# A gated linear scan with a feed-forward layer: a list scheduler that counts TensorE's changes of mode and searches 1,000 orders

## The chip, the cores and the metric

The kernel runs on one core of one Trainium2 chip. The core has five engines that run side by side, each strictly in the order of its own instruction list: TensorE (PE, matrix products; its weight loads are listed apart as PEld), VectorE (DVE, elementwise work and scans), ScalarE (ACT, activation functions and copies), GpSimd (POOL) and SyncE (SP, which here issues every transfer). An instruction waits until the data it reads is there, and everything behind it on the same engine waits too. The metric is the time of one execution on the device in microseconds. The kernel before took 576.96, 577.83 and 579.1 us in three runs, median 577.83.

## The reference, cut to what matters

```python
# 4 batches, 8 heads, 768 positions, head size 48
scale = np.minimum(mag, 0.999) / (mag + 1e-06)       # mag = |a_re + i a_im|
a_re_n, a_im_n = (a_re * scale, a_im * scale)
for t in range(S):                                    # a gated state of 48x48 per head
    new_re = ar * S_re - ai * S_im
    new_im = ar * S_im + ai * S_re
    S_re, S_im = (new_re + k[t] v[t]^T, new_im)
    y[t] = q[t] @ S_re
x = y reshaped to 3072 tokens x 384
h = x @ w_in                                          # 384 -> 2048
g = np.where(h >= 1, h, np.where(h <= -1, 0.0, (h + 1) ** 2 / 4))
out = g @ w_out                                       # 2048 -> 384
```

All inputs and the output are float32.

## The kernel before, in words

**Tiling.** The 3072 tokens are cut into 12 units of 256 tokens (`u`). A unit passes three steps. `gates(u)` turns the gates into running log-magnitudes and angles and multiplies them into keys and queries; this is DVE and ACT work, and its last two products per unit (`turn`, line 834 before) write the tiles `x` and `kq`, whose rows are then moved to the per-head tiles `hd` by ten transfers (`spread`). `attend(u)` does the scan in chunks of 128 tokens on PE: `scores` (line 989, tile `sc`), `transposes` (933, `tp`), `products` (962, `dp`) and `values` (1030 and 1038, `yp`). DVE multiplies the scores by a mask (997, `am`); ACT copies `yp` to `xr` (1050), and six small transfers per unit move rows inside `xr`. `moe(blk)` is the feed-forward layer for a block of two units. `split` rounds `xr` into a high part `xH` (ACT, 1130) and a rest `xL` (DVE, 1137); `gemm1` (1160) multiplies with `w_in` into `h`, `gemm2` (1235) with `w_out` into `o`, each product as three matmuls of 128x512 (high-high, low-high, high-low). Between the two, ACT makes `s` (1185, and for the first two blocks also 1195 and 1199) and DVE makes `g` (1204, later also 1212); `gh` (ACT, 1218) and `gl` (DVE, 1222) are its two parts. The weights arrive packed and are unpacked on the way (`weights`: DVE lines 431, 440, 449, 460, ACT line 455). Attention of the later units is woven into the feed-forward work of the block before, in visits of a few matmuls.

**Width.** `values` and `products` run PE on 64 of its columns (the forms 96x64 and 128x64 in the profile), everything else on 128. Going from one to the other is what the change calls a change of mode.

**What sets the order.** Nothing is written out by hand. Every piece of work is recorded with `Plan.op`: its engine, a cost in ns, what it reads and writes, and, for some, a due time. `Plan.order` first walks backwards through the dependences, so that each piece gets the latest due time that its successors allow (DVE and ACT costs are taken 1.6 times for that). Then it plays the list forward once on five engines: the engine that is free first takes, among what is ready, the piece with the earliest due time. All pieces are emitted in the order of their planned starts. Tiles are single buffers with fixed places, so a writer also waits for the readers of the tile that lay there before.

**Fillers.** Where the plan shows a gap on PE ahead of the feed-forward part, `warm` puts matmuls into it whose result nobody reads (line 1290, `idle`; 85% of the planned gap at 224 ns for each).

Of the kernel before, what the change touches and what calls it, by code (L numbers as in the profile page):

```python
# [3 lines left out]

# [16 lines left out]
NH = 8  # L21
# [7 lines left out]
CH = 128  # L29
# [53 lines left out]
LO_PE = 3  # L83
INFLATE = 1.6
SPLIT_DUE = 3000


def key_rows():
# [36 lines left out]
class Plan:  # L125
# [3 lines left out]
    def __init__(self):  # L129
        self.ops = []  # L130
        self.slots = {}
        self.glued = {}
        self.loose = set()

    def tile(self, slot, make):
        t = Tile_(make, self.slots.get(slot))
        self.slots[slot] = t
        return t

    def op(self, eng, cost, fn, r=(), w=(), due=None, dma=0, after=(), glue=None, late=0):  # L140
        i = len(self.ops)
        pre = set(after)
# [24 lines left out]
        return i  # L167

    def order(self):
        ops = self.ops  # L170
        n = len(ops)
        succ = [[] for _ in range(n)]
        for i, o in enumerate(ops):
            for p in o[3]:
                succ[p].append(i)
        due = [0.0] * n
        big = 1e12
        for i in range(n - 1, -1, -1):
            eng, cost, _, _, d, dma, late = ops[i]
            t = big if d is None else d  # L180
# [4 lines left out]
            for s in succ[i]:  # L185
                t = min(t, due[s] - own)
            due[i] = t
        left = [len(o[3]) for o in ops]
        ready = [0.0] * n
        end = [0.0] * n  # L190
        start = [0.0] * n
        free = {e: 0.0 for e in ("PE", "DVE", "ACT", "SP", "POOL")}
        wait = {e: [] for e in free}
        avail = {e: [] for e in free}
        queue = {}

        def enable(i):
            heapq.heappush(wait[ops[i][0]], (ready[i], i))

        for i in range(n):  # L200
            if not left[i]:
                enable(i)
        done = 0
        taken = set()
        forced = []
        while done < n:
            if forced:
                i = forced.pop()
                e = ops[i][0]
                t = max(free[e], ready[i])  # L210
            else:
                best = None
                for e in free:
                    while avail[e] and avail[e][0][1] in taken:
                        heapq.heappop(avail[e])
                    while wait[e] and wait[e][0][1] in taken:
                        heapq.heappop(wait[e])
                    if avail[e]:
# [42 lines left out]
            for s in succ[i]:  # L261
                left[s] -= 1
                lat = LAT[eng]
                if dma or s in self.loose:
                    lat = 0
                elif ops[s][0] == eng:
                    lat = SAME[eng]
                ready[s] = max(ready[s], end[i] + lat)
                if not left[s]:
                    enable(s)  # L270
# [3 lines left out]
        self.start, self.end, self.due = start, end, due  # L274
        return sorted(range(n), key=lambda i: (start[i], i))

    def emit(self, warm):
        order = self.order()
# [43 lines left out]
def gated_scan_moe(  # L322
# [575 lines left out]
    def attend(u):  # L898
# [25 lines left out]
        def transposes(c):  # L924
            cs = slice(c * CH, (c + 1) * CH)
            out = []
            for g in range(2):
                TP = bank([P, 4, HR], f"tp_{u}_{g}_{c}")
                KT = pl.tile(f"kT{g}", lambda g=g: keys[g])

                def run(g=g, TP=TP):
                    for i, h in enumerate(GROUPS[g]):
                        PE_.transpose(TP.get()[:, i, :], head(h)[:, 0, cs], ident[:HR, :HR])  # L933

                def tail(TP=TP, KT=KT):
# [10 lines left out]
                out.append((4 * 83, run, [hd[h // 3] for h in GROUPS[g]], TP, tail))  # L946
                carry.setdefault("kT", []).append(KT)
            return out

        def products(c):  # L950
# [23 lines left out]
                    fn = lambda: V_.tensor_tensor(ST.get(), old.get(), DP.get()[:HR], op=ALU.add)  # L974
                pl.op("DVE", dve(DM), fn, r=[DP] + ([old] if old else []), w=[ST])

            return [(NH * 124, run, [*kT, V_c[0]], DP, tail)]

        def scores(c):
            cs = slice(c * CH, (c + 1) * CH)  # L980
            out, ams = [], []
            for g in range(2):
# [21 lines left out]
                        w=[AM],  # L1004
                    )

                out.append((4 * pe32(CH), run, [hd[h // 3] for h in GROUPS[g]], SC, tail))
                ams.append(AM)
            return out, ams

        def values(c, ams, st):
# [5 lines left out]
            def part(prs):  # L1017
# [59 lines left out]
        def visit(parts):  # L1077
            reads = [x for p in parts for x in p[2]]
            last = None
            for n, (cost, run, r, psum, tail) in enumerate(parts):  # L1080
# [499 lines left out]
```

## Time and profile before

| | |
|---|---|
| three timed runs | 576.96, 577.83, 579.1 us |
| span of the profiled execution | 575.6 us, 9984 instructions |
| what lies around the span, against the median of the runs | 2.2 us |
| PE busy | 561.4 us (98%), 3922 matmuls |
| DVE busy | 434.5 us (75%) |
| ACT busy | 406.1 us (71%) |
| mean granted PE clock | 0.998 |

The page gives the busy share of each engine over the whole span, and the same in 40 slices. An average of 75% for DVE hides that it is nearly full early on and half idle at the end, so the span is best read stage by stage. A matmul's row counts from its start to its modelled end, and matmuls overlap: what a matmul costs is the distance from its start to the next one's start (for 128x512 some 0.23 us), not the 0.39 us of its row.

### The profile page before, as it was taken

What the parts mean: (1) busy time and instruction counts of PE and PEld (TensorE: products, weight loads), DVE (VectorE), ACT (ScalarE), POOL (GpSimd) and SP (SyncE); (2) the same over time, 40 slices, a digit from 0 to 9 for tenths busy, and PEclk for the clock granted to TensorE, in tenths of its full rate; (3) what the DMA queues carried; (4) which work ended last, traced back from release to release, by engine and by line L of the source; (5) the groups of instructions that cost most, each with busy time, mean ns of one, the idle gap of its engine ahead of it and who ended that gap; (6) DMA issues with size and microseconds to landing.
All of it is one profiled execution on the core that took longest, in us unless ns stands there. A gap on an engine that the chain in (4) does not pass through costs nothing.

```text
span 575.6 us, 9984 instructions
## 1 busy us (share of the span) xinstructions
PE 561.4 (98%) x3922; PEld 478.4 (83%) x3922; DVE 434.5 (75%) x625; ACT 406.1 (71%) x654; POOL 1.7 (0%) x20
## 2 busy tenths in 40 slices
PE   8999999999999999999999999999999999999995
PEld 7798978888888888888888888888888888888883
DVE  4999999999979498579589878887885544455452
ACT  7776799887998998975576666667643333369972
POOL 1000000000000000000000000000000000000000
PEclk9999999999999999999999999999999999999999
DMA  8676571773641614712601613402312200078811
GB/s 352 250 198 192 163 262 55 192 282 114 188 173 48 195 68 125 237 57 82 174 2 52 202 56 102 153 2 85 114 56 72 74 1 7 21 265 309 298 42 61
DMA packets 23527, 77.42 MB, mean 134 GB/s; under 512 B 4528, under 2 KB 10288, under 8 KB 23472
## 3 DMA queue, kind: packets, MB, share of 16 engines
q1 hardware_dynamic: 23472, 76.70, 40.8%
q8 instruction: 33, 0.54, 0.4%
q14 instruction: 22, 0.18, 0.1%
HBM read 51.90 MB, written 4.72 MB: 98 GB/s over the span
## 4 chain that ended last, share of the span: by engine, by line
PE 78%; DVE 12%; ACT 5%; DMA 2%; issue 1%; SPq 0%; ACTq 0%; DVEq 0%
PE o L1235 30%; PE h L1160 29%; PE sc L989 6%; PE yp L1038 3%; PE yp L1030 3%; PE dp L962 2%; PE tp L933 1%; PE idle L1290 1%; ACT ai L608 1%; DVE kq L725 1%; DMA xr<-xr 1%; DMA ai<-in_art_dram 1%; DVE g L1204 1%; ACT x L608 1%; DVE raw_i L440 1%
## 5 line engine op out<-in xcount | busy, mean ns | idle before, releaser
L1160 PE MATMUL h<-xH,wi 128*128 128x512 f32 x576 | 180.6, 395 | 1.2 <-DVE g L1204 0.9
L1235 PE MATMUL o<-gh,wo 128*128 128x512 f32 x576 | 180.4, 394 | 0.0
L1160 PEld LDWEIGHTS h<-xH,wi 128*128 128x128 f32 x576 | 106.2, 188 | 22.6 <-DVE g L1204 1.1
L1235 PEld LDWEIGHTS o<-gh,wo 128*128 128x128 f32 x576 | 106.3, 188 | 21.6 <-issue 0.7
L1204 DVE TENSOR_TENSOR g<-h,s 128x512 f32<-128x512 f32 x96 | 65.9, 687 | 63.1 <-ACT s L1185 45.6
L1160 PE MATMUL h<-xL,wi 128*128 128x512 f32 x288 | 112.6, 391 | 0.0
L1235 PE MATMUL o<-gl,wo 128*128 128x512 f32 x288 | 112.5, 391 | 0.0
L1185 ACT ACTIVATE s<-h,cst 128x512 f32<-128x512 f32 x96 | 65.7, 685 | 42.0 <-PE h L1160 38.9
L1218 ACT CAST gh<-g 128x512 fp32r<-128x512 f32 x96 | 59.1, 616 | 46.0 <-DVE g L1212 43.6
L1222 DVE TENSOR_TENSOR gl<-g,gh 128x512 fp32r<-128x512 f32 x96 | 66.0, 687 | 31.9 <-ACT gh L1218 31.8
L1160 PEld LDWEIGHTS h<-xL,wi 128*128 128x128 f32 x288 | 54.1, 188 | 12.1 <-DVE xL L1137 0.4
L1235 PEld LDWEIGHTS o<-gl,wo 128*128 128x128 f32 x288 | 54.1, 188 | 11.6
L608 ACT ACTIVATE ai<-ai 128x768 f32<-128x768 f32 x49 | 41.2, 843 | 19.1 <-DVE ai L777 8.6
L989 PE MATMUL sc<-hd 96*128 96x128 f32 x384 | 49.6, 278 | 0.0
L989 PEld LDWEIGHTS sc<-hd 96*128 96x128 f32 x384 | 47.0, 192 | 2.2
L1212 DVE SCALAR_TENSOR_TENSOR g<-s,g 128x512 f32<-128x512 f32 x64 | 44.2, 691 | 1.8
L1038 PE MATMUL yp<-am,V 128*64 128x128 f32 x384 | 35.5, 273 | 0.2 <-DVE am L997 0.2
L997 DVE TENSOR_TENSOR am<-sc,sums 128x512 f32<-128x512 f32 x48 | 32.5, 683 | 3.1 <-PE sc L989 2.8
L1290 PE MATMUL idle<-sums,ident 128*128 128x128 f32 x238 | 31.3, 291 | 1.7 <-POOL sums masks.py:66 1.7
L1030 PE MATMUL yp<-hd,st 96*64 96x128 f32 x320 | 32.1, 278 | 0.3 <-DVE am L997 0.3
L1290 PEld LDWEIGHTS idle<-sums,ident 128*128 128x128 f32 x238 | 30.3, 206 | 2.5 <-POOL sums masks.py:66 1.7
L402 ACT ACT_TABLE_LOAD x21 | 26.9, 1283 | 0.4
(104 smaller groups left out, 651.6 us busy)
## 6 DMA issues: line engine op xcount, KB each, us to landing
chk<-in_wl_dram SPq DMA_DIRECT2D x16, 768.0 KB, 5.2
kq<-in_kq_dram SPq DMA_DIRECT2D x12, 768.0 KB, 4.7
ai<-in_ari_dram SPq DMA_DIRECT2D x10, 768.0 KB, 6.1
hd<-x SPq DMA_DIRECT2D x24, 288.0 KB, 4.1
hd<-kq SPq DMA_DIRECT2D x24, 288.0 KB, 4.9
raw_i<-in_wl_dram SPq DMA_DIRECT2D x8, 768.0 KB, 4.6
raw_o<-in_wl_dram SPq DMA_DIRECT2D x8, 768.0 KB, 5.8
V<-in_v_dram SPq DMA_DIRECT2D x12, 384.0 KB, 3.2
```

What stands on the lines that cost most here:

```text
L608: lambda: A_.activation(out(), src(), f, **kw),
L989: PE_.matmul(SC.get()[:, i, :], t[:, 0, cs], t[:, 1, cs], start=True, stop=True)
L1030: PE_.matmul(o_, st.get().rearrange("p h e -> p (h e)")[:, lo : lo + 64], head(h)[:, 1, cs], start=True, stop=False,)
L1038: PE_.matmul(o_, V.get()[:, c, lo : lo + 64], ams[pr // 2].get()[:, 2 * (pr % 2) + e, :], start=st is None, stop=True,)
L1160: PE_.matmul(H.get(), weight["i", f // 2].get()[:, f % 2, part, sl], x.get()[:, j, :], start=j == 0 and n == 0, stop=j == NJ - 1 and n == 2,)
L1185: lambda: A_.activation(SS.get(), H.get(), AF.Relu, bias=c_half, scale=-0.5 if spare else 0.5),
L1204: lambda: V_.tensor_tensor(G.get(), H.get(), SS.get(), op=ALU.max),
L1212: lambda: V_.scalar_tensor_tensor(G.get(), SS.get(), 1.0, G.get(), op0=ALU.min, op1=ALU.mult),
L1218: pl.op("ACT", act(T), lambda: A_.copy(GH.get(), G.get()), r=[G], w=[GH])
L1222: lambda: V_.tensor_tensor(GL.get(), G.get(), GH.get().bitcast(F32), op=ALU.subtract),
L1235: PE_.matmul(PO[m].get(), weight["o", f // 2].get()[:, f % 2, part, sl], g.get(), start=f == 0 and n == 0, stop=f == NF - 1 and n == 2,)
L1290: PE_.matmul(idle["h1"], ident, mask, start=True, stop=True)
```

## The change

`op` gets a flag `narrow`, set for `values` and `products`. In the forward pass (now `forward`) a PE piece that differs in width from the one before costs 140 ns more going to narrow and 212 ns more going back; flat surcharges in the old costs (400 ns for some `values`, 60 ns at the end of a visit, a factor of 0.92) go away. A new pass `backward` plays the list from its end and so gives every piece another due time. `order` then makes 1,000 rounds with a seeded random generator: each round either mixes in due times of the backward pass or shifts the due times of one to ten pieces near one moment, plays the list forward again, and keeps the new due times if the planned end is earlier or, with a chance that falls over the rounds, if it is a little later. The best plan seen is emitted. The work itself, the tiles and the rules of `warm` are as before.

```diff
+TO_NARROW, TO_WIDE = 140, 212
+ROUNDS, SEED = 1000, 0
+REACH = (100e3, 180e3, 300e3, 600e3)
...
+    def forward(self, due):
...
             start[i] = t
+            if eng == "PE":
+                if narrow != (i in self.narrow):
+                    narrow = not narrow
+                    cost += TO_NARROW if narrow else TO_WIDE
+            took[i] = cost
             free[e] = t + cost
...
+    def backward(self, plan):
...
+        total = max(end)
+        return [total + d for d in due]
+
+    def order(self):
...
+        due = self.first_due()
+        plan = self.forward(due)
+        best = (max(plan[1]), due, plan)
+        cost = best[0]
+        rng = random.Random(SEED)
+        for k in range(ROUNDS):
+            part = rng.random()
+            if k == 0 or part < 0.15:
+                share = 1.0 if k == 0 else rng.random()
+                new = [a + (b - a) * share for a, b in zip(due, self.backward(plan))]
+            else:
+                new = list(due)
+                t = rng.uniform(0, rng.choice(REACH))
+                w = rng.choice((1e3, 5e3, 15e3, 40e3))
+                eng = rng.choice(("DVE", "ACT", "PE", "SP", "DVE", "ACT", None))
+                near = [
+                    i
+                    for i, a in enumerate(plan[0])
+                    if abs(a - t) < w and (eng is None or ops[i][0] == eng)
+                ]
+                shift = rng.choice((500, 2000, 6000, 15000))
+                for i in rng.sample(near, min(rng.choice((1, 1, 2, 3, 5, 10)), len(near))):
+                    new[i] += rng.gauss(0, shift)
+            trial = self.forward(new)
+            value = max(trial[1])
+            heat = 300.0 * (1 - k / ROUNDS) + 6.0
+            if value <= cost or rng.random() < math.exp((cost - value) / heat):
+                cost, due, plan = value, new, trial
+                if cost < best[0]:
+                    best = (cost, due, plan)
...
-            return [(NH * 124, run, [*kT, V_c[0]], DP, tail)]
+            return [(NH * 116, run, [*kT, V_c[0]], DP, tail, True)]
...
-                return ((4 if st else 2) * len(prs) * 110 + (400 if prs[0] == 0 else 0), run, r, Y, tail)
+                return ((4 if st else 2) * len(prs) * 110, run, r, Y, tail, True)
...
-                cost = 0.92 * cost + (60 if n == len(parts) - 1 else 0)
-                last = pl.op("PE", cost, run, r=reads if n == 0 else r, w=[psum], glue=last)
+                last = pl.op("PE", cost, run, r=reads if n == 0 else r, w=[psum], glue=last, narrow=narrow)
```

Three places show how the order moves. Line numbers of the changed kernel are 98 or 99 higher than before; the last number of a tile's name only counts tiles.

**DVE, ahead of the first feed-forward matmul.** The two `am` rows are the mask products of unit 1, the last attention work that block 0 needs; `x_319` and `kq_465` (after: `x_313`, `kq_462`) are unit 2's turned keys and queries, `wi`/`wo` are rests of unpacked weights, `xL` is the split of block 0. Before:

```order
L725 TENSOR_TENSOR kq_465<-kq_465,x_319 128x1536
L972 COPY st_0_605<-dp_0_579 96x384
L786 TENSOR_SCALAR state<-ai_107 128x3
L460 TENSOR_TENSOR wo_518<-raw_o_231,wo_518 128x2x384
L997 TENSOR_TENSOR am_0_1_615<-sc_0_1_598,sums 128x512
L997 TENSOR_TENSOR am_1_1_625<-sc_1_1_609,sums 128x512
L834 TENSOR_TENSOR x_319<-kq_465,ai_107 128x1536
L834 TENSOR_TENSOR kq_465<-kq_465,ai_107 128x1536
L1137 TENSOR_TENSOR xL_687<-xr_447,xH_661 128x3x256
```

After:

```order
L824 TENSOR_TENSOR kq_462<-kq_462,x_313 128x1536
L559 TENSOR_TENSOR wi_518<-raw_i_280,wi_518 128x2x384
L933 TENSOR_TENSOR x_313<-kq_462,ai_111 128x1536
L1071 COPY st_0_628<-dp_0_598 96x384
L1096 TENSOR_TENSOR am_0_1_637<-sc_0_1_620,sums 128x512
L1096 TENSOR_TENSOR am_1_1_647<-sc_1_1_632,sums 128x512
L721 TENSOR_TENSOR ai_468<-ai_468 128x768
L933 TENSOR_TENSOR kq_462<-kq_462,ai_111 128x1536
L530 TENSOR_SCALAR y_o_688<-raw_o_501 128x768
L735 SCALAR_TENSOR_TENSOR x_626<-ai_468,x_626 128x3x256
L1235 TENSOR_TENSOR xL_712<-xr_454,xH_649 128x3x256
```

Counted from the start of the list to the last of these `am` rows, the changed list has exactly two more DVE instructions than before: one weight rest (`wi`) and unit 2's `x`. All others are the same in number, though partly in another order.

**SP, the same place.** The transfers into `xr` are the last thing that block 0 waits for. Before:

```order
L392 DMA hd_0_658<-x_319 48x1536
L392 DMA hd_1_663<-x_319 48x1536
L392 DMA hd_2_683<-x_319 32x1024
L392 DMA xr_447<-xr_447 16x256 x6
L392 DMA hd_0_658<-kq_465 48x1536
```

After:

```order
L491 DMA hd_2_630<-x_313 16x512
L491 DMA hd_0_640<-x_313 48x1536
L491 DMA hd_1_651<-x_313 48x1536
L491 DMA hd_2_630<-x_313 32x1024
L491 DMA hd_2_630<-x_313 16x512
L491 DMA hd_0_640<-kq_462 48x1536
L491 DMA xr_454<-xr_454 16x256 x6
L491 DMA hd_1_651<-kq_462 48x1536
```

Six of unit 2's transfers now stand ahead of them in place of three, and the sixth reads `kq`, which DVE makes behind the last `am`.

**ACT, at the first feed-forward results.** `s_0` are the three steps from the first `h` to the first `g`. Before:

```order
L1130 CAST xH_661<-xr_447 128x256
L608 ACTIVATE x_685<-x_685,cst 128x3x256
L455 CAST wo_763<-raw_o_622 128x2x384
L1185 ACTIVATE s_0_768<-h_0_737,cst 128x512
L1195 ACTIVATE s_0_768<-s_0_768,cst 128x512
```

After:

```order
L1228 CAST xH_649<-xr_454 128x256
L554 CAST wo_726<-raw_o_501 128x2x384
L1228 CAST xH_649<-xr_454 128x256 x2
L707 ACTIVATE x_626<-x_626 128x3x256
L1283 ACTIVATE s_0_785<-h_0_752,cst 128x512
L1293 ACTIVATE s_0_785<-s_0_785,cst 128x512
```

The cast of a weight has moved from just ahead of `s_0` to between the last casts of `xH`.

On PE the list of real work ahead of the first feed-forward matmul is the same set, with 128 fillers in it in place of 119. Over the main program PE goes from 128 to 64 columns 24 times and back 24 times, 20 and 20 of these behind the first feed-forward matmul, in both lists. Attention work breaks into the feed-forward matmuls 52 times before and 51 times after. The last rows of every engine, behind the last `gemm2`, are the same.

More of the change, by code (lines that the diff above doesn't have):

```diff
@@ L2 @@
 import math
+import random
 from contextlib import ExitStack
@@ L138, in tile, with op @@
         return t
-    def op(self, eng, cost, fn, r=(), w=(), due=None, dma=0, after=(), glue=None, late=0):
+    def op(self, eng, cost, fn, r=(), w=(), due=None, dma=0, after=(), glue=None, late=0, narrow=False):
         i = len(self.ops)
+        if narrow:
+            self.narrow.add(i)
         pre = set(after)
@@ L167, in op, with first_due @@
         return i
-    def order(self):
+    def first_due(self):
         ops = self.ops
[L171 to L178, printed above, removed]
+        due = [0.0] * len(ops)
+        for i in range(len(ops) - 1, -1, -1):
             eng, cost, _, _, d, dma, late = ops[i]
-            t = big if d is None else d
+            t = 1e12 if d is None else d
             if dma:
@@ L184, in order, with lag @@
                 own = cost * (INFLATE if eng in ("ACT", "DVE") else 1.0) + LAT[eng]
-            for s in succ[i]:
+            for s in self.succ[i]:
                 t = min(t, due[s] - own)
             due[i] = t
+        return due
+    def lag(self, i, s):
+        eng, dma = self.ops[i][0], self.ops[i][5]
+        if dma or s in self.loose:
+            return 0
+        return SAME[eng] if self.ops[s][0] == eng else LAT[eng]
+    def forward(self, due):
+        ops = self.ops
+        n = len(ops)
         left = [len(o[3]) for o in ops]
@@ L191, in order @@
         start = [0.0] * n
+        took = [o[1] for o in ops]
         free = {e: 0.0 for e in ("PE", "DVE", "ACT", "SP", "POOL")}
@@ L195, in order @@
         queue = {}
-        def enable(i):
-            heapq.heappush(wait[ops[i][0]], (ready[i], i))
         for i in range(n):
             if not left[i]:
-                enable(i)
+                heapq.heappush(wait[ops[i][0]], (ready[i], i))
         done = 0
@@ L205, in order @@
         forced = []
+        narrow = False
         while done < n:
@@ L260, in order @@
             done += 1
-            for s in succ[i]:
+            for s in self.succ[i]:
                 left[s] -= 1
[L263 to L268, printed above, removed]
+                ready[s] = max(ready[s], end[i] + self.lags[i, s])
                 if not left[s]:
-                    enable(s)
+                    heapq.heappush(wait[ops[s][0]], (ready[s], s))
             nxt = self.glued.get(i)
@@ L273, in order @@
                 forced.append(nxt)
-        self.start, self.end, self.due = start, end, due
-        return sorted(range(n), key=lambda i: (start[i], i))
+        return start, end, took
+    def backward(self, plan):
+        ops = self.ops
+        n = len(ops)
+        start, end, took = plan
+        left = [len(s) for s in self.succ]
+        tail = [0.0] * n
+        free = {e: 0.0 for e in ("PE", "DVE", "ACT", "SP", "POOL")}
+        wait = {e: [] for e in free}
+        avail = {e: [] for e in free}
+        moved = 0.0
+        due = [0.0] * n
+        for i in range(n):
+            if not left[i]:
+                heapq.heappush(wait[ops[i][0]], (0.0, i))
+        for _ in range(n):
+            best = None
+            for e in free:
+                if avail[e]:
+                    t = free[e]
+                elif wait[e]:
+                    t = max(free[e], wait[e][0][0])
+                else:
+                    continue
+                if best is None or t < best[0]:
+                    best = (t, e)
+            t, e = best
+            while wait[e] and wait[e][0][0] <= t:
+                _, i = heapq.heappop(wait[e])
+                heapq.heappush(avail[e], (-start[i], i))
+            _, i = heapq.heappop(avail[e])
+            dma, late = ops[i][5:]
+            if dma:
+                moved = max(tail[i], moved) + dma
+                t = max(moved + DMA_FIX + DMA_END + late, free[e] + took[i])
+                free[e] += took[i]
+            else:
+                t += took[i]
+                free[e] = t
+            due[i] = -t
+            for p in ops[i][3]:
+                left[p] -= 1
+                tail[p] = max(tail[p], t + self.lags[p, i])
+                if not left[p]:
+                    heapq.heappush(wait[ops[p][0]], (tail[p], p))
+        total = max(end)
+        return [total + d for d in due]
@@ new lines, in order @@
+    def order(self):
+        ops = self.ops
+        n = len(ops)
+        self.succ = [[] for _ in range(n)]
+        for i, o in enumerate(ops):
+            for p in o[3]:
+                self.succ[p].append(i)
+        self.lags = {(i, s): self.lag(i, s) for i in range(n) for s in self.succ[i]}
+        due = self.first_due()
[8 more added lines that the diff above has]
+                new = [a + (b - a) * share for a, b in zip(due, self.backward(plan))]
+            else:
+                new = list(due)
[17 more added lines that the diff above has]
+                    best = (cost, due, plan)
+        _, self.due, (self.start, self.end, took) = best
+        for o, t in zip(ops, took):
+            o[1] = t
+        return sorted(range(n), key=lambda i: (self.start[i], i))
@@ L944, in tail @@
                     )
-                out.append((4 * 83, run, [hd[h // 3] for h in GROUPS[g]], TP, tail))
+                out.append((4 * 83, run, [hd[h // 3] for h in GROUPS[g]], TP, tail, False))
                 carry.setdefault("kT", []).append(KT)
@@ L1005, in tail @@
                     )
-                out.append((4 * pe32(CH), run, [hd[h // 3] for h in GROUPS[g]], SC, tail))
+                out.append((4 * pe32(CH), run, [hd[h // 3] for h in GROUPS[g]], SC, tail, False))
                 ams.append(AM)
@@ L1079, in visit @@
             last = None
-            for n, (cost, run, r, psum, tail) in enumerate(parts):
-                cost = 0.92 * cost + (60 if n == len(parts) - 1 else 0)
-                last = pl.op("PE", cost, run, r=reads if n == 0 else r, w=[psum], glue=last)
+            for n, (cost, run, r, psum, tail, narrow) in enumerate(parts):
+                last = pl.op("PE", cost, run, r=reads if n == 0 else r, w=[psum], glue=last, narrow=narrow)
                 visits.append((len(todo_visits), last))
```

1 line of the change is left out of this document (added).

## The prediction

> **What bounds the kernel now.** First the busy time of each engine in three stretches, cut at the first feed-forward matmul (70.41 us) and at the end of the last one (568.28 us). The columns are the stretch, its length, and the busy time of PE, PEld, DVE, ACT and POOL:
>
> ```profile
> 0.00:70.41 70.41, 64.67 (x624) 59.62 (x625) 59.81 (x80) 51.46 (x74) 1.65 (x20) 1.00 0.68 232
> 70.41:568.28 497.87, 496.64 (x3298) 418.77 (x3298) 374.36 (x544) 354.04 (x580) 0.00 (x0) 1.00 0.37 121
> 568.28:575.60 7.32, 0.12 (x2) 0.01 (x2) 0.29 (x2) 0.58 (x1) 0.00 (x0) 0.86 0.37 120
> ```
>
> The middle is PE alone: 496.64 of 497.87 us busy, so feeding PE better can win 1.23 us there at the most. The list of waits names them:
>
> ```profile
> PE h L1160 <- DVE g L1204: 0.9, 1, 0.9
> PE yp L1030 <- DVE am L997: 0.3, 1, 0.3
> ```
>
> The last 7.3 us are the output's way out, whose rows do not move. What is left is the head: when does the first `h` start? PE is no measure there, since its 64.67 busy us hold the fillers. By slices of 24 us, DVE (the third time) is the full engine:
>
> ```profile
> 24.00:48.00 24.00, 22.11 (x197) 19.70 (x195) 23.34 (x32) 16.33 (x24) 0.00 (x0) 1.00 0.63 178
> 48.00:72.00 24.00, 23.59 (x311) 22.35 (x310) 22.99 (x32) 18.34 (x28) 0.00 (x0) 1.00 0.52 168
> 72.00:96.00 24.00, 23.07 (x169) 19.43 (x168) 23.62 (x35) 22.79 (x35) 0.00 (x0) 1.00 0.42 157
> ```
>
> The end of the head, in order of time, from the timelines of DVE, PE, ACT and SP:
>
> ```profile
> 57.17 1.75 DVE L725 TENSOR_TENSOR kq<-kq,x 128x1536 f32<-128x1536 f32 x1
> 58.84 0.55 DVE L972 COPY st<-dp 96x384 f32<-96x384 f32 x1
> 60.24 1.28 DVE L997 TENSOR_TENSOR am<-sc,sums 128x512 f32<-128x512 f32 x2
> 63.21 1.76 DVE L834 TENSOR_TENSOR kq<-kq,ai 128x1536 f32<-128x1536 f32 x1
> 67.55 0.94 DVE L460 TENSOR_TENSOR wi<-raw_i,wi 128x768 fp32r<-128x768 f32 x1
> 68.42 0.55 DVE L431 TENSOR_SCALAR y_o<-raw_o 128x768 uint32<-128x768 uint32 x1
> 62.13 1.28 ACT L402 ACT_TABLE_LOAD   x1
> 64.32 0.48 ACT L1050 COPY xr<-yp 128x384 f32<-128x384 f32 x1
> 63.20 1.79 SPq L392 DMA_DIRECT2D hd<-x  x3
> 65.10 4.75 SPq L392 DMA_DIRECT2D xr<-xr  x6
> 65.89 4.04 DMA xr<-xr
> 70.41 0.73 PE L1160 MATMUL h<-xH,wi 128*128 128x512 f32 x2 [0.26 <-ACT xH L1130]
> ```
>
> The last masks of unit 1 end at 61.52 (60.24 + 1.28). `values` and the copy to `xr` follow, SP issues six moves from 65.10, the second lands 4.04 us after its issue, ACT rounds, and `h` starts: 8.89 us from the last mask to `h`, with DVE the gate ahead of it.
>
> **The change, part by part.** *The head.* Two DVE instructions now stand ahead of the last mask that stood behind it: unit 2's `x` (128x1536) and a weight rest (128x768). From start to start the first kind takes 58.84 - 57.17 = 1.67 us, the second 68.42 - 67.55 = 0.87 us, together 2.54 us. Some of it may fall into DVE's idle spots before the last mask, which the groups of DVE from 8 to 61 us show at the end of each row:
>
> ```profile
> L636 DVE SCALAR_TENSOR_TENSOR x<-ai,x 128x768 f32<-128x768 f32 x3 | 2.9, 955 | 1.3 <-ACT ai L608 1.3
> L684 DVE COPY state<-dec 128x2 f32<-128x2 f32 (+1 forms) x4 | 0.6, 155 | 0.5 <-ACT x L695 0.5
> L725 DVE TENSOR_TENSOR kq<-kq,x 128x1536 f32<-128x1536 f32 x3 | 5.3, 1753 | 0.4 <-ACT x L695 0.4
> L737 DVE TENSOR_SCALAR ai<-turns 128x512 int32<-128x512 f32 (+1 forms) x4 | 2.2, 552 | 0.3 <-ACT ai L608 0.3
> ```
>
> These are 2.5 us, all waits for ACT's first steps on the first two units, and they lie before 30 us, where the two moved instructions cannot run; only a smoother order there gives some back. So the two rows are bounded by 0 (all of it given back) and +2.54. From the last mask to `h` something is saved too: before, the table load (62.13) and a cast kept ACT from the second copy of `xr` for about 0.2 us; in the new order the load stands well before. I take **+2.0 us** for the head, near the full price, because DVE idles less than 0.7 us in all between 24 and 48 us; ends +0.5 and +3.0 (with half a microsecond for the SP queue, below).
>
> *The moved transfers.* Three more `hd` transfers go ahead of the six `xr` moves. SP's own rows price an issue at 1.79 / 3 = 0.6 us, so 1.8 us in all, if SP were late. Five of the six read `x`, which is now made before the last mask, so they are issued while PE still works on `values`; the sixth needs `kq`: last mask at 61.52 + 2.54 = 64.06, an `ai` row (0.87) and `kq` (1.76) behind it give 66.7. The moves themselves are ready at 65.10 + 2.54 - 0.2 = 67.4. After 0.6 for the sixth issue that is a cover of 0.1 us: I count 0, and what it costs without cover is the slow rival below.
>
> *The first wait in the middle.* Before, `h` waited at 77.64 for `g`, and `g` for the three ACT steps on the first `h`, which began late behind a weight's cast:
>
> ```profile
> 73.89 0.90 ACT L455 CAST wo<-raw_o 128x768 fp32r<-128x768 f32 x1 [0.26 <-DVE raw_o L449]
> 74.69 0.68 ACT L1185 ACTIVATE s<-h,cst 128x512 f32<-128x512 f32 x1
> 76.16 0.63 ACT L1199 ACTIVATE s<-s 128x512 f32<-128x512 f32 x1
> 76.90 0.68 DVE L1204 TENSOR_TENSOR g<-h,s 128x512 f32<-128x512 f32 x1
> 77.64 0.73 PE L1160 MATMUL h<-xH,wi 128*128 128x512 f32 x2 [0.93 <-DVE g L1204]
> ```
>
> The cast now stands two places earlier, and four transposes more stand on PE ahead of the waiting `h`. The chain starts up to 0.9 us sooner, which is all of this wait. Of the 1.23 us of waits I take **-1.0**; ends -1.23 and +1.5. The upper end is one DVE row of 1.67 us in front of some `g` or mask, less a little, in the stretch to 96 us where DVE has 0.4 us to spare: no row shows such a wait, but a list that was searched until its planned gaps closed has no slack left that would absorb one.
>
> *The changes of mode.* The price is on PE's rows (start to start; a plain step of two 128x512 matmuls is 102.89 - 102.44 = 0.45):
>
> ```profile
> 102.44 0.62 PE L1235 MATMUL o<-gh,wo 128*128 128x512 f32 x2
> 102.89 0.39 PE L1235 MATMUL o<-gl,wo 128*128 128x512 f32 x1
> 103.21 0.44 PE L1030 MATMUL yp<-hd,st 96*64 96x128 f32 x4
> 106.04 0.74 PE L1235 MATMUL o<-gh,wo 128*128 128x512 f32 x2
> 106.62 0.40 PE L1235 MATMUL o<-gl,wo 128*128 128x512 f32 x1
> ```
>
> Going to 64 columns takes 0.32 in place of about 0.23, so 0.09 more; coming back 0.58 in place of 0.45, so 0.13 more: 0.22 a pair, where the planner now charges 0.352. But the new list has as many changes as the old (20 and 20 behind the first `h`): this term is **0**. One visit fewer (51 for 52) is worth 0.1 at those prices: **-0.1**.
>
> *The end.* Same rows behind the last `o`: 0.
>
> The sum: 575.6 + 2.0 - 1.0 - 0.1 = **576.5 us of span**, 0.9 more than before. With the 2.2 us that lay between the span and the median, the median would be **578.7 us**, against 577.83. What this measurement cannot tell from no change is 0.5%, or 2.9 us; so I forecast no change that can be measured.
>
> **Rivals.** *The head gets shorter.* With unit 2's `x` made early, its transfers are out of the way sooner, and the moves into `xr` no longer queue behind them. The group of rows of `xr` between 60 and 72 us gives what such a move takes without company:
>
> ```profile
> DMA to landing us min/median/max: 1.8/3.2/4.6
> ```
>
> If the deciding one fell from 4.04 to 1.8, and the two DVE rows vanished in the 2.5 us of idle time, the head would shrink by 2.2, and with all 1.23 us of waits gone the span is 572.1, the median 574.4 (0.6% faster). For it: five of the six transfers do go early. Against it: the sixth, a large one, goes directly ahead of the moves, and the masks stand behind more work. Chance 0.07.
>
> *SP's queue turns.* The place is the sixth `hd` transfer ahead of the `xr` moves. It decides from the point where `kq` on DVE ends later than the copies of `xr` on ACT; the cover is 0.1 us by the sum above. Then SP waits for `kq` with the six moves behind it, and each microsecond of DVE's lateness goes straight into the start of `h`. Price: 0.6 for the issue, one DVE row more ahead of `kq` (1.67), and a landing at 4.6, the longest of that group, in place of 4.04: 2.8. With a head of +2.54 and no gain from the waits the span is 575.6 + 2.54 + 2.8 = 580.9, the median 583.1 (0.9% slower). Chance 0.10, since the cover is thin.
>
> *New waits in the middle.* If two DVE rows like the 1.67 one come in front of `g` rows between 72 and 144 us, PE waits 3.3 us: 575.6 + 2.0 + 3.3 = 580.9 again. Against it: DVE was as full before (23.62 of 24 us from 72 to 96), and PE waited 1.23 us in all. Chance 0.05.
>
> *PE's clock falls.* In the last stretch PE has nothing to do for 7.3 us, and the granted clock means 0.86 there in place of 1.00. If the fillers (21 now ahead of `h`, 23 before) ended early and left PE idle, the next matmuls would run slower. That 0.86 over 7.32 us is at most 1.0 us of lost clock; the same loss at the start of `h` gives 577.5 and a median of 579.7, still no change. Chance 0.02. The Trainium skill (TensorE: Matmul & The Clock Gate, "Part 1: The HAM clock gate") says that the clock halves after an idle window of about 3.4 us; this trace has one such place, the last stretch, and agrees in kind. By that rule the loss would come only from a wait of that length, longer than any PE wait listed here (0.9 us).
>
> *The change does not do what it says:* of fewer changes of mode that is already so in the list, and it stands in the forecast as 0.
>
> **How the numbers follow.** Forecast 0.76, rivals 0.07, 0.10, 0.05 and 0.02. Faster by over 0.5% is the first rival, 0.07; slower the second and third, 0.15; the same 0.76 + 0.02 = 0.78. The forecast's own ends are 575.6 + 0.5 - 1.23 - 0.1 = 574.8 and 575.6 + 3.0 + 1.5 = 580.1 of span, so 577.0 and 582.3 of median, which rarely meet. For the range I take 575.5 to 582.0: below, the runs before spread 0.9 us under their median and the first rival reaches down to 574.4; above, it takes in nearly all of the forecast's upper end and stops short of 583.1.
>
> **What would show it.** In the profile after: the first `h` at 72.4 (71 to 73.5); the last mask of unit 1 ending near 64; the second `xr` move issued near 68; the wait of `h` for `g` gone or under 0.3 us; the stretch from the first `h` to the last `o` 496.8 long; the tail 7.3. Wrong would be a first `h` before 70.4 (then DVE was not the gate), or one after 74 with SP waiting for `kq`, or more than 1.5 us of PE waits in the middle.

## The result, and the profile after

The changed kernel takes 583.98 us (median of five runs, 583.03 to 587.99), the kernel before 579.10 us beside it (576.96 to 580.45). The ratio is 1.0103 with a 95% interval of 1.0069 to 1.0138: slower by 1.0%, where 578.7 us and no change were forecast, and above the end of the range, 582.0.

The profiled execution took 583.03 us, with a span of 581.3 against 575.6. Its three stretches (the columns as in the prediction):

```profile
0.00:73.42 73.42, 67.17 (x643) 61.78 (x643) 61.87 (x82) 53.30 (x76) 1.65 (x20) 1.00 0.71 239
73.42:573.80 500.38, 497.28 (x3298) 418.22 (x3298) 370.34 (x542) 352.44 (x578) 0.00 (x0) 1.00 0.37 118
573.80:581.30 7.50, 0.12 (x2) 0.01 (x2) 0.29 (x2) 0.58 (x1) 0.00 (x0) 0.76 0.37 117
```

So the 5.7 us are 3.0 of head (73.42 for 70.41), 2.5 of the middle (500.38 for 497.87) and 0.2 of tail. Behind the first `h` PE has the same 3298 matmuls as before, so whatever the head loses can be won back only from PE's waits, 1.2 us in all. The list of PE's waits behind the first `h` says what the middle lost:

```profile
PE o L1333 <- ACT gh L1316: 2.3, 1, 2.3
PE h L1258 <- ACT xH L1228: 0.6, 1, 0.6
PE h L1258 <- DVE g L1302: 0.5, 1, 0.5
PE o L1333 <- DVE gl L1320: 0.4, 1, 0.4
```

The second row is the head's own. The wait of `h` for `g` did shrink, from 0.93 to 0.49, but `o` now waits 2.25 + 0.35 us for `gh` and `gl`, which it never did before. The timeline there:

```profile
201.34 0.62 PE L1333 MATMUL o<-gh,wo 128*128 128x512 f32 x2
202.00 0.62 ACT L1316 CAST gh<-g 128x512 fp32r<-128x512 f32 x1 [3.20 <-PE o L1333]
202.66 0.69 DVE L1320 TENSOR_TENSOR gl<-g,gh 128x512 fp32r<-128x512 f32 x1 [3.72 <-PE o L1333]
206.20 0.60 ACT L1316 CAST gh<-g 128x512 fp32r<-128x512 f32 x1
206.85 0.73 PE L1333 MATMUL o<-gh,wo 128*128 128x512 f32 x2 [2.25 <-ACT gh L1316]
207.94 0.50 PE L1333 MATMUL o<-gl,wo 128*128 128x512 f32 x1 [0.35 <-DVE gl L1320]
```

Read it from the bottom. PE is idle for 2.25 us because the second `gh` comes at 206.20; that one is late because ACT stood still for 3.20 us in front of the first `gh`; and ACT stood still for **PE**, for an `o`. ACT's cast reads `g` and no `o`: a writer that waits for the engine that will read it waits for a buffer. Here are the orders of PE and ACT at this place (block 1; the digit behind `gh` and `h` is `f`, the one behind `o` the third of the output, the last number only counts tiles):

```
PE   L1333 MATMUL o_0_1846<-gh_5_2004,wo_726 128x512 x2
PE   L1088 MATMUL sc_0_0_2052<-hd_0_1926 128x128
...
PE   L1258 MATMUL h_8_2070<-xL_1655,wi_904 128x512
PE   L1333 MATMUL o_1_1838<-gh_3_1934,wo_322 128x512 x2
...
PE   L1333 MATMUL o_1_1838<-gh_4_1982,wo_726 128x512 x2
...
PE   L1333 MATMUL o_0_1846<-gh_6_2057,wo_949 128x512 x2
ACT  L1316 CAST gh_6_2057<-g_6_2042 128x512
```

`gh` and `gl` share six buffers, so `f` 6 writes where `f` 3 lay, and `o_1<-gh_3`, the last reader of that one, now stands behind the scores and the three groups of `h_8`. Does the planner know? It takes the readers of the former tile at the moment at which the writer is recorded, and `moe` records the groups of `h` and `gh` of `f` **before** the groups of `o` of `f` - 3. Those readers are then not there yet, and the dependence is missing from the plan; only on the chip is it kept. In the order before, due times happened to put every such reader ahead of its writer, by 1.8 us or more in the planner's own times. In the changed plan `gh` of `f` 6 starts at 195.23 us, while the last reader of its buffer runs from 198.94 to 199.63.

The end of the head, from the timelines of DVE, ACT, SP and PE:

```profile
62.92 1.27 DVE L1096 TENSOR_TENSOR am<-sc,sums 128x512 f32<-128x512 f32 x2
64.98 1.75 DVE L933 TENSOR_TENSOR kq<-kq,ai 128x1536 f32<-128x1536 f32 x1
66.96 0.62 ACT L1149 COPY xr<-yp 128x128 f32<-128x128 f32 x2
66.90 0.62 SPq L491 DMA_DIRECT2D hd<-kq  x1
67.62 4.50 SPq L491 DMA_DIRECT2D xr<-xr  x6
72.96 0.40 ACT L1228 CAST xH<-xr 128x256 fp32r<-128x256 f32 x1 [3.92 <-DMA xr<-xr]
73.42 0.73 PE L1258 MATMUL h<-xH,wi 128*128 128x512 f32 x2 [0.59 <-ACT xH L1228]
```

The last masks end at 64.19 (62.92 + 1.27), 2.7 us later than before, `xr` moves from 67.62, and `h` starts 9.2 us behind the last mask (8.89 before).

### The profile page after: what moved, and what is told of

It is laid out like the page before. It is cut to its first block, busy times and chain, and to the rows that moved or that the text cites. A ratio compares the mean times of both kernels' runs of the same rounds, so it can differ in the third digit from the quotient of the medians.

```text
span 581.3 us, 10056 instructions
## 1 busy us (share of the span) xinstructions
PE 564.6 (97%) x3940; PEld 480.0 (83%) x3940; DVE 432.5 (74%) x625; ACT 406.3 (70%) x654; POOL 1.6 (0%) x20
## 4 chain that ended last, share of the span: by engine, by line
PE 86%; DVE 4%; DMA 3%; ACT 3%; SPq 1%; issue 1%; ACTq 0%; DVEq 0%
PE o L1333 34%; PE h L1258 34%; PE sc L1088 7%; PE yp L1137 3%; PE yp L1129 3%; PE dp L1061 3%; PE tp L1032 2%; DMA raw_i<-in_wl_dram 1%; DMA xr<-xr 1%; SPq L491 1%; ACT ai L707 1%; DMA hd<-kq 1%; PE dec L764 0%; DVE raw_i L548 0%; DVE x L735 0%
## 5 line engine op out<-in xcount | busy, mean ns | idle before, releaser
L1388 PE MATMUL idle<-sums,ident 128*128 128x128 f32 x256 | 33.2, 292 | 1.7 <-POOL sums masks.py:66 1.7
L1388 PEld LDWEIGHTS idle<-sums,ident 128*128 128x128 f32 x256 | 32.3, 207 | 2.3 <-POOL sums masks.py:66 1.7
```

What stands on the lines that cost most here:

```text
L1388: PE_.matmul(idle["h1"], ident, mask, start=True, stop=True)
```

## The experiments

Two questions: is the wait near 207 us the buffer, and what makes the head late? Beside them, which half of the change is to blame, the prices or the search. In runs 1, 2, 3 and 5 the changed kernel's planner runs as it is, and instructions are then moved in its list. The numbers together, each with the kernel before on the same chip beside it (first `h`, and the stretch from there to the end of the last `o`, are of the profiled execution):

| | median us | ratio to before (95%) | first `h` | stretch |
|---|---|---|---|---|
| before | 578.06 to 579.10 | 1 | 70.41 | 497.87 |
| changed | 583.98 | 1.0103 (1.0069 to 1.0138) | 73.42 | 500.38 |
| 1 readers of the buffer earlier | 581.48 | 1.0051 (1.0028 to 1.0074) | 75.05 | 497.09 |
| 2 DVE's `x` behind the mask | 585.04 | 1.0121 (1.0091 to 1.0151) | 73.17 | 502.41 |
| 3 both | 580.57 | 1.0035 (1.0018 to 1.0052) | 73.51 | 497.68 |
| 4 new prices, no search | 581.44 | 1.0053 (1.0033 to 1.0073) | 71.86 | 500.54 |
| 5 head of before, 1 behind it | 584.04 | 1.0118 (1.0091 to 1.0146) | 69.97 | 503.65 |
| 6 `o` recorded first, search | 580.41 | 1.0040 (1.0020 to 1.0060) | 72.01 | 497.09 |
| 7 search, old prices | 580.66 | 1.0029 (1.0007 to 1.0050) | 70.19 | 501.30 |
| 8 as 7, `o` first, longer | 578.69 | 1.0005 (0.9984 to 1.0025) | 71.44 | 497.34 |
| 9 measured prices, no search | 579.71 | 1.0024 (1.0010 to 1.0039) | 71.62 | 498.54 |
| 10 measured prices, `o` first, longer | 581.31 | 1.0035 (1.0012 to 1.0058) | 77.02 | 495.47 |

(In run 10 the stretch holds 20 matmuls fewer than in the others, 3278; they stand ahead of the first `h`.)

### 1. The readers ahead of the scores

```diff
-ROUNDS, SEED = 1000, 0
+ROUNDS, SEED, MOVES = 1000, 0, ((689, 693), (701, 689))
-        order = self.order()
+        order = moved(self.order(), MOVES)
+def moved(order, moves):
+    for i, j in moves:
+        order.remove(i)
+        order.insert(order.index(j) + 1, i)
+    return order
```

(689 and 701 are `o_1<-gh_3` and `o_1<-gh_4`; 693 is the last group of `h_7`.)

> The changed kernel's order, with two of PE's 288 groups of o moved: the groups of row m=1 of f 3 and f 4 of block 1, which in the changed order stand behind the scores and the three groups of h of f 8, come ahead of the scores and of the o group in front of them. They are the last readers of the buffers of gh and gl that f 6 and f 7 write. Theory B (the buffer): ACT's 3.2 us and DVE's 3.7 us of waiting for PE near 202 us are the wait for these readers, so they fall below 0.5 us, PE's 2.3 + 0.4 us near 207 us go too, the stretch from the first h to the last o falls from 500.4 to 497.2 to 498.0 us, and the kernel takes 580.5 to 581.7 us. Rival L (lateness): ACT and DVE are behind anyway at that point and the wait only names the last of many; PE's wait stays within 1 us of 2.7 us and the time within 0.5 us of 584.0 us.

The list of PE's waits behind the first `h` of this run, and its stretch from 192 to 216 us; the row by itself is that stretch in the changed kernel:

```profile
PE h L1258 <- ACT xH L1228: 0.8, 1, 0.8
PE h L1258 <- DVE g L1302: 0.5, 1, 0.5
192.00:216.00 24.00, 24.00 (x175) 20.52 (x174) 17.30 (x25) 22.64 (x38) 0.00 (x0) 1.00 0.39 127
```

```profile
192.00:216.00 24.00, 21.39 (x155) 17.09 (x153) 14.86 (x22) 18.66 (x32) 0.00 (x0) 1.00 0.31 106
```

Neither ACT nor DVE waits for PE's `o` there any more, PE is busy for all 24 us again, and the ratio falls from 1.0103 to 1.0051. No instruction was taken away and no other engine's list was touched, so the wait was the buffer: it is about half of the loss. (The stretch of 497.09 is just under what was expected; the late first `h` of this execution is one of clock, of which below.)

### 2. One DVE row back behind the mask

```diff
+MOVES = ((181, 134), (182, 181), (183, 182), (184, 183), (185, 147), (186, 185), (188, 186))
```

(`moved` is as in 1; 181 is unit 2's `x`, 134 the last mask of unit 1; 182 to 186 and 188 are SP's transfers of `hd`, 147 the last move of `xr`.)

> The changed kernel's order, with the head half undone: DVE's row of x of unit 2 (L933, 1.67 us) comes behind the last mask of unit 1, and the transfers on SP that follow from it stand as before the change (three of hd from x, the six of xr, then the others of hd). The decoding row of wi (L559, 0.87 us) stays ahead of the mask. Theory D (the DVE rows set the head): the last mask ends 1.67 us sooner (64.2 to 62.5 us), the first h starts near 71.7 us (71.3 to 72.0 us), 1.4 to 2.1 us sooner than 73.4 us, and the time is 581.9 to 582.9 us. Rival Q (the queue alone sets it): the same gain of the mask, but the first h gains no more than the 0.6 us of the one transfer that is taken out of the way. The wait near 207 us stays under both.

Both theories fell: the first `h` came at 73.17, 0.25 sooner, and the mask hardly moved. The timelines of DVE and ACT in this run:

```profile
62.25 0.69 DVE L1096 TENSOR_TENSOR am<-sc,sums 128x512 f32<-128x512 f32 x1 [0.52 <-PE sc L1088]
63.40 0.69 DVE L1096 TENSOR_TENSOR am<-sc,sums 128x512 f32<-128x512 f32 x1 [0.45 <-PE sc L1088]
64.00 1.75 DVE L933 TENSOR_TENSOR x<-kq,ai 128x1536 f32<-128x1536 f32 x1
66.65 0.85 ACT L707 ACTIVATE ai<-ai 128x768 f32<-128x768 f32 x1 [1.32 <-DVE ai L721]
68.38 0.62 ACT L1149 COPY xr<-yp 128x128 f32<-128x128 f32 x2
```

With 1.67 us less ahead of it, DVE waits for the scores, and the masks end at 64.09 (64.19 before the edit). The scores were late by themselves. Why, the chain of waits shows; before:

```profile
50.38 1.81 PE sc L989 x16
52.20 0.37 PE yp L1030 x4
```

and in the changed kernel:

```profile
51.18 1.81 PE sc L1088 x16
53.00 0.66 PE tp L1032 x8
53.66 0.70 PE rest_o L568 x2
54.53 0.37 PE yp L1129 x4
```

PE's `values` of the first chunk stand 2.3 us later. Of this 1.2 us come in between: eight transposes and a weight rest are new in this place, four other transposes have left it. The other 1.1 were there before: the `values` ahead start at 46.86 for 45.73, after waits of PE for the transfer of `hd` (0.56) and for a mask (1.08 for 0.82), and after another weight rest. And the row that was put back returned in another: `x` ahead of `ai` makes ACT wait 1.32 us with the copies of `xr` behind it (66.96 in the changed kernel, 68.38 here). So the head is late on DVE, PE and ACT at once, and no single row is its price.

### 3. Both edits

```diff
+MOVES = ((689, 693), (701, 689), (181, 134), (182, 181), (183, 182), (184, 183), (185, 147), (186, 185), (188, 186))
```

> The two edits together: the two groups of o moved ahead of the scores, and x of unit 2 behind the last mask with SP's transfers as before. If the buffer and the head are the two causes and add up, the first h starts near 71.7 us, the stretch from there to the last o is 497.2 to 498.0 us, and the kernel takes 578.6 to 580.2 us, within 0.4% of the kernel before. If something else in the changed order costs time (the prices, the rest of the order), it stays above 581.5 us.

580.57 us lies between the two cases. The stretch of 497.68 is the one expected of the buffer, the first `h` (73.51) is near that of the second run: the edit of the head brings no earlier `h`. What is left, 0.35% or 2.0 us, goes with a head that is still 3.1 us late, and this edit doesn't show what makes it so.

### 4. The prices without the search

```diff
-ROUNDS, SEED = 1000, 0
+ROUNDS, SEED = 0, 0
```

> The changed planner with its new prices and no search (no rounds): the list scheduler runs once with the first due times. Theory S (the search makes the loss): the due times keep the writers of gh and gl behind the readers, ACT waits for PE nowhere by more than 1 us between the first h and the last o, and the time is 577 to 581 us. Rival P (the prices make it): the time is 582 us or more, as with the search.

581.44 us fell between them, and theory S in part with it: the prices alone, played once, cost 0.5%. No writer of `gh` waits for PE here, which agrees with S; the loss is a later first `h` (71.86) and one wait, which stood at 0.93 before, with a slower PE clock behind it (last section):

```profile
PE h L1258 <- DVE g L1302: 1.7, 1, 1.7
```

Beside the changed kernel this run shows what the search was paid for. By the planner's own times, at the same prices, the search moved the first `h` from 70.06 to 71.12 us, shortened the stretch from there to the last `o` from 501.9 to 498.4, and so ended 2.5 us earlier. On the chip the stretch is 500.54 here and 500.38 with the search, the first `h` 1.6 us later with it, and the ratio to before 1.0103 for 1.0053: the later head was real, and most of what it bought was not.

### 5. The head of before

```diff
+HEAD_OPS = (...)
+def ahead(order):
+    return list(HEAD_OPS) + [i for i in order if i not in HEAD_SET]
-        order = self.order()
+        order = ahead(moved(self.order(), MOVES))
```

(The first 278 instructions of the order before, with its fillers; `MOVES` as in 1.)

> The order of the kernel before up to the end of the first six groups of h (278 instructions), then everything else in the changed order, with the two groups of o moved ahead of the scores in block 1. The run with the mask freed of one DVE row showed that no single row sets the head: the mask, the scores and the last copies of xr are later on DVE, PE and ACT alike. Theory T (trade): the changed order did rows of units 2 and 3 in the head that the order before does later, so with the head of before the first h starts at 70.0 to 70.9 us, but those rows then stand in front of the next h or the transposes, and PE waits 2 to 5 us in all between 72 and 90 us (1.2 us before); the time is 580 to 583 us, about that of the run with the two groups moved alone (581.5 us). Rival N (the later head bought nothing): the first h is at 70.0 to 70.9 us, PE waits no more than 1.5 us from there to the last o, and the time is 577 to 579 us.

The first `h` starts at 69.97, 3.5 us before that of the changed kernel, and PE then waits 5.0 us:

```profile
PE tp L1032 <- DVE am L1096: 4.4, 1, 4.4
PE h L1258 <- DVE g L1302: 0.6, 1, 0.6
```

DVE's timeline ahead of that mask:

```profile
78.63 0.56 DVE L530 TENSOR_SCALAR y_i<-raw_i 128x768 uint32<-128x768 uint32 x1 [1.49 <-DMA raw_i<-in_wl_dram]
79.11 0.95 DVE L559 TENSOR_TENSOR wo<-raw_o,wo 128x768 fp32r<-128x768 f32 x1
79.98 0.95 DVE L539 SCALAR_TENSOR_TENSOR raw_i<-raw_i,y_i 128x768 uint32<-128x768 uint32 x1
80.97 0.96 DVE L548 SCALAR_TENSOR_TENSOR raw_i<-raw_i 128x768 uint32<-128x768 uint32 x1
81.84 1.28 DVE L1096 TENSOR_TENSOR am<-sc,sums 128x512 f32<-128x512 f32 x2
```

The waits are those of theory T (584.04 us is above its range, with PE's slower clock, last section, as a part), and so is the mechanism: the changed order unpacks a weight ahead of these masks, because its head issued that load at 61.45; the head of before issues it at 74.07, DVE waits 1.49 us for it, and four rows stand ahead of the mask. But the run says less than it seems. The order before has its masks ahead of that weight, so the 4.4 us belong to the join of two orders and are no price of the early head in its own order. What the run shows is that a head and what follows were planned together; that the changed order's head is worth its 3.0 us, it does not show. The sum speaks against it: run 1 has no wait left but 0.5 us, and the 0.5% (2.9 us) by which it is still behind is about the head's 3.0.

### 6. `o` recorded ahead of `h`

```diff
         for k in range(NF + LAG):
+            if k >= LAG:
+                gemm2(k - LAG)
             if k < NF:
                 gemm1(k)
-            if k >= LAG:
-                gemm2(k - LAG)
```

> The changed planner with two lines of moe exchanged: the groups of o of f - 3 are recorded before the groups of h of f, so that the writers of gh and gl know the readers of the tiles that had their buffers, and the search of 1,000 trials runs with those dependences. Theory B (the buffer that the planner didn't see): no wait of ACT or DVE for PE above 1 us between the first h and the last o, PE waits less than 1.5 us there, and the time falls from 584.0 to 579.0 to 581.5 us; what is left over the kernel before is the head (the first h at 72 to 74 us). Rival: the search finds another place that the chip doesn't keep, PE waits 2 us or more at a new place, and the time stays above 582.5 us.

As theory B has it. PE's only wait listed behind the first `h`:

```profile
PE tp L1032 <- DVE am L1096: 0.6, 1, 0.6
```

No writer of `gh` or `gl` waits for an `o`, the first `h` is at 72.01, the median 580.41. This is the repair in the planner itself, and it is worth as much as the repair by hand.

### 7. The search with the old prices

```diff
-TO_NARROW, TO_WIDE = 140, 212
+TO_NARROW, TO_WIDE = 0, 0
...
```

(and the old costs of `values`, `products` and visits.)

> The search of 1,000 trials with the prices of before (no price for a change of mode, the old costs of the attention's groups), nothing else changed: the half of the change that the run without a search left out. If the new prices are what makes the later head (that run had the first h at 71.9 us and a wait of 1.75 us near 80 us with no search at all), this one starts the first h at 69.5 to 71 us, waits less than 1.5 us after it, and takes 576.5 to 578.5 us, the kernel before or a little under it. If the search itself makes the loss, by wearing down the slack between writers and readers, ACT waits for PE by more than 2 us somewhere and the time is 580 us or more.

The head is as the first case has it (70.19), the time is not (580.66). It is in the range of the second case, but not for its reason: no writer of `gh` or `gl` waits for an `o` here. The search made another wait that the plan doesn't hold, near 296 us; from the list of waits and the chain:

```profile
PE dp L1061 <- ACT kT L1038: 2.0, 1, 2.0
```

```profile
283.98 0.53 SPq L491
284.55 5.81 DMA xr<-xr
290.46 0.04 ACT xH L1228
295.68 0.39 ACT kT L1038
296.11 1.14 PE dp L1061 x32
```

The last of six 16 KB moves of `xr` was put directly behind the load of the next `kq` (768 KB) on SP. It landed 5.8 us after its issue, where the six of that place have a median of 2.8 and the plan had 4.0 for this one. ACT stood for it, and everything behind on ACT was late.

### 8. Old prices, `o` first, a longer search

As 6 and 7 together, with 4,000 rounds, seed 2 and `REACH = (75e3, 90e3, 180e3, 600e3)`.

> The search with the prices of before, the two lines of moe exchanged as above, 4,000 trials and more of the shifts in the first 90 us (seed 2). This is the version that the reading so far points to: the first h at 70 to 71 us and no PE wait above 0.7 us after it; 576.3 to 577.8 us, 0.05 to 0.3% under the kernel before. If prices don't matter for the head, it is no better than the search with the new prices, 579 us or more.

578.69 us beside 578.67: the kernel before again, and no better: the first `h` is at 71.44 where 70 to 71 was expected, and a wait is 0.99 us where 0.7 was the most. Neither case of the expectation holds. It is the best of the ten, and no version here beats the kernel before.

### 9. and 10. Prices as measured

```diff
-TO_NARROW, TO_WIDE = 140, 212
+TO_NARROW, TO_WIDE = 92, 110
-            return [(NH * 116, run, [*kT, V_c[0]], DP, tail, True)]
+            return [(NH * 126, run, [*kT, V_c[0]], DP, tail, True)]
-                return ((4 if st else 2) * len(prs) * 110, run, r, Y, tail, True)
+                return ((4 if st else 2) * len(prs) * 114, run, r, Y, tail, True)
```

9 has no search; 10 has the exchange of 6, 4,000 rounds, seed 2 and `REACH = (75e3, 75e3, 90e3, 180e3)`.

> No search, as in the run with the new prices alone, but the prices are those that the traces show: 92 and 110 ns for the two changes of mode instead of 140 and 212, and groups of the attention that are 3.6% and 8.6% longer instead of the change's figures. If wrong sizes of the prices are what makes the order worse without a search (first h at 71.9 us, a wait of 1.75 us near 80 us, 0.5% over the kernel before), right ones bring the first h to 70.4 to 71.2 us, the wait under 1.1 us, and the time to 577 to 579.5 us. If the list scheduler's order is simply shifted by any change of prices, the time stays at 580.5 to 582.5 us.

> The search with the measured prices, the two lines of moe exchanged, 4,000 trials and most shifts in the first 90 us (seed 2). If the given prices are what keeps the search above the kernel before (0.4% with the two lines exchanged), this run comes to 577 to 579 us with no PE wait above 0.7 us after the first h. If the start from which the search begins decides, it stays at 579.5 us or more, as the search with the given prices (580.4 us), and only the start from the old prices (578.7 us) reaches the kernel before.

Without a search the measured prices take the loss from 0.53% to 0.24%; 579.71 is just outside either case. The wait of `h` for `g` is 0.5 instead of 1.75, the first `h` (71.62) stays late. With a search, 581.31 us is the second case: right prices don't help it. This order puts the first `h` at 77.02 and waits for nothing afterwards, but PE stands 2.0 us ahead of it:

```profile
PE h L1258 <- ACT xH L1228: 2.0, 1, 2.0
```

Why every list that starts from priced changes of mode comes out 0.2 to 0.5% above the kernel before is not settled. Part of the later head is in the plan already: by its own times the planner starts the first `h` at 70.06 us with either set of prices (runs 4 and 9), and at 68.99 before. Runs 4 and 9, one order each, suggest that the sizes of the prices matter too; their intervals overlap. What is shown is that nothing was won by the prices anywhere.

## Why the prediction was wrong

**The step that failed is "The first wait in the middle".** Its -1.0 us of PE waits became +1.9 (3.09 behind the first `h` for 1.19), and more than 1.5 us of such waits was the prediction's own sign of being wrong. Of the 4.8 us by which the span missed (581.3 for 576.5) this term is 2.9, the head 1.0, the rest of the middle 0.7, the end 0.2. The old waits did shrink, but by 0.7 (the one of 0.93 to 0.49, not under 0.3). What the step missed is a new one, at 207 us and not in the stretch to 96 us, on `gh` and not on DVE. The sentence on a list "searched until its planned gaps closed" looked for lost slack on DVE; the slack that mattered lay between the reader and the next writer of a buffer, and neither the profile before nor a count of rows shows it. It could have been read: six buffers, the order of PE against that of ACT, and the rule by which a writer learns of readers. The rival "New waits in the middle" had the right kind and price (3.3 us), the wrong place, and 0.05.

**The head** was forecast at +2.0 and came at +3.0, the upper end. The mask was forecast at 64.06 and ended at 64.19, and still the reason did not hold: by run 2, taking one of the two DVE rows away moves the mask by 0.1 us, since PE's scores are as late by their own list. Two engines were late by the same amount, and the sum had priced one; that its number for the mask came out is in part luck. The gain of half a microsecond from the mask to `h` did not come: 9.2 us for 8.89, with `ai` rows ahead of ACT's copies. What the earlier rows were to buy, fewer waits in the middle, could never be more than 1.2 us.

**The moved transfers** went as written: `hd` from `kq` issued at 66.90, the moves of `xr` from 67.62 (forecast 67.4), the second of them at 68.22 (68), the thin cover held, and the rival "SP's queue turns" did not happen. **The changes of mode** were counted at 0. Without its waits the stretch is 497.3 us (500.38 - 3.09), before 496.7 (497.87 - 1.19), in run 6 496.4 (497.09 - 0.65): no gain in it. The 0.6 us that the changed order has more are gone in run 1 too, whose busy time there is 496.57 (497.28 in the changed kernel, 496.64 before), so they belong to the same place as the wait. **The end** is 7.5 for 7.3.

**"PE's clock falls"** had 0.02, on the ground that no PE wait listed before was longer than 0.9 us. The new one is 2.25 us, and in other runs waits of that length were followed by a slower clock; see the last section. "The head gets shorter" had nothing for it in the end.

**From span to median** 2.2 us were taken over; here it is 583.98 - 581.3 = 2.7, for the profiled execution was the quickest of the five.

## What to carry to other kernels

A search over orders drives a plan to the edge of its model, so each dependence or shared resource that the model leaves out, and that slack covered so far, will be found by it: check the searched order against the buffers' readers and the transfers' queue before trusting the planned end. When a row is moved ahead of a stage that several engines fill, ask who else is late by as much: taking that row away again is worth only the difference. On a kernel whose PE is busy for 496.6 of 497.9 us, a better order has 1 us to win in the middle and several to lose.

## What the runs showed of the hardware

Waits of PE of about 2 us were followed by a slower PE clock. The rows are stretches of 4 us with the granted clock behind the busy times of five engines, for run 4 (the wait of 1.75 us ends at 79.8), run 2 (waits of 2.26 and 0.32 us that end at 207.4 and 208.4), run 7 (1.95 us, to 296.1) and run 10 (2.0 us, to 77.0):

```profile
76.00:80.00 4.00, 2.25 (x18) 2.02 (x18) 3.93 (x7) 3.76 (x7) 0.00 (x0) 1.00 0.63 195
80.00:84.00 4.00, 4.00 (x11) 3.11 (x11) 3.38 (x6) 3.96 (x6) 0.00 (x0) 0.57 0.89 329
84.00:88.00 4.00, 4.00 (x24) 3.33 (x23) 4.00 (x6) 3.03 (x6) 0.00 (x0) 1.00 0.20 83
```

```profile
208.00:212.00 4.00, 3.69 (x11) 2.85 (x11) 3.97 (x7) 3.06 (x5) 0.00 (x0) 0.58 0.01 2
```

```profile
296.00:300.00 4.00, 3.89 (x43) 3.64 (x44) 3.19 (x5) 2.33 (x5) 0.00 (x0) 0.68 0.02 4
300.00:304.00 4.00, 4.00 (x17) 3.21 (x17) 4.00 (x8) 3.08 (x4) 0.00 (x0) 0.89 0.01 2
```

```profile
76.00:80.00 4.00, 2.98 (x10) 2.36 (x11) 3.00 (x8) 2.85 (x6) 0.00 (x0) 0.82 0.81 298
80.00:84.00 4.00, 4.00 (x25) 3.06 (x26) 3.96 (x6) 2.94 (x6) 0.00 (x0) 0.75 0.65 267
```

Each time 1.7 us of clock are lost (4 x 0.43; 4 x 0.42; 4 x 0.32 + 4 x 0.11; 4 x 0.18 + 4 x 0.25), as by half a clock for 3.4 us. Such a wait thus costs nearly twice its length. Around run 5's wait of 4.40 us, to 82.58, 3.4 us of clock are lost (0.51 from 80 to 84 and 0.63 from 84 to 88), a part of it while PE still waited. A slower clock doesn't follow every wait: in the changed kernel's profile, PE's 2.25 us to 206.85 and 1.56 us to 14.39 left the next rows at 1.00. That execution had a mean clock of 0.997 and 583.03 us, the four others 0.992 to 0.994 and 583.88 to 587.99; a loss of 1.7 us is 0.003 of the span, so it is likely, though not seen, that they had it. In the profiles of the kernel before and of runs 3, 6, 8 and 9, whose PE waits from the first `h` on reach 1.04 us at most, the clock stayed at 1.00 up to 552 us. In run 1 the dip fell into the head, around and behind a wait of 2.96 us that ends at 14.71,

```profile
16.00:20.00 4.00, 4.00 (x19) 3.64 (x19) 2.88 (x6) 2.64 (x6) 0.00 (x0) 0.62 1.01 418
```

and the twelve `dec` matmuls behind it take 3.30 us for 2.20 in the changed kernel. Its first `h` stands 1.6 us behind that of the changed kernel, whose head it shares row by row.

The Trainium skill (TensorE: Matmul & The Clock Gate, "Part 1: The HAM clock gate") has the clock halve after an idle window of about 3.4 us. The size and kind agree with these rows; the length doesn't, since waits of 1.75 to 2.26 us were enough here, and the measurement decides.
